# Packed attention and a SoLU layer: batch 1's Z from float16 halves, a new order of the steps, more unread matmuls

## The chip, the cores and the metric

The kernel runs on one core of a Trainium2 chip. The metric is the device time of one execution in microseconds. Three runs of the kernel before took 389.59 to 392.84 us, with a median of 391.43.

## The reference

Eight batches of eight heads attend twice: 32 packed queries to 576 keys, then 576 queries to the 32 packed rows. The result, 4608 tokens of 512 values, goes through a layer with SoLU and a layer norm. All arrays are float32.

```python
p_packed = sm_attn(p, k, v)            # softmax(p k^T / 8) v, per batch and head
x = sm_attn(q, p_packed, p_packed)     # then (tokens, heads * 64)
h = x @ w_in                           # 512 -> 1024
solu = h * softmax(h)
ln = (solu - mean) / sqrt(var + 1e-06) * g_ln
out = ln @ w_out                       # 1024 -> 512
```

## The kernel before

The second attention and the first layer are one product here: for each batch b, Z is the packed rows times w_in (`make_z`, steps z0 to z7), and h is the second softmax times Z. Every product of the token tiles runs on TensorE (PE) in float16 with a high and a low half of each operand and three of the four cross terms.

A batch takes these flows. `pack` (steps k) transposes the keys, takes scores, maximum and exponential, transposes the exponentials, multiplies by v and leaves the packed rows, transposed, with their size. `unpack` (q) does the second softmax and leaves its high and low half, a_h and a_l. `make_z` (z) leaves the two halves zh and zl of Z. Batch 0 and 1 turn keys and queries on PE (`transpose_pairs`), the others on VectorE (DVE). The 4608 tokens are 36 tiles of 128 (`token_tile`, t0 to t35): a product of 12 matmuls for h, then maximum, exponential, u = e h, mean, a high and a low half of the centred u, a transposing DMA (yT, issued by SyncE's queue, SP), and a product of 24 matmuls with w_out's halves wch and wcl in four steps, an eviction scaled by the row's norm, and a store.

The preparation reads w_in in four parts (load `lw`, conversion W) and w_out in four (`lo`, O), turns p (steps p) and g (`lg`, g), finds the size of the weights (N, S) and scales w_out's halves (C). In `make_z`, `ZP_BY` says for each batch how the product is made: '0' from float32 operands (L570), '1' from float16 halves of the packed rows and of w_in (L564, three terms). Batches 0 and 1 use float32 before, the others halves. The halves of w_in come from `weight_halves` (steps H): a high half per part on ScalarE (ACT, L342) and a low half per part on DVE (L344), written over the float32 w_in, so float32 products must be over first.

Two flows make matmuls that nobody reads: `warm_up` (Z) ahead of the first transposes and `keep_clock` (X), two matmuls of 384 columns in each of four steps.

Each flow is a Python generator, and a step is what lies between two `yield`s. The string `ORDER` names the flow whose next step is issued, 1316 names in all; the kernel issues in this order, so it fixes the order of the instructions on every engine and on SP's queue. The engines run their own instructions in that order and wait for each other by semaphores. Strings such as `SOFT_BY`, `A2L_BY`, `SCALED_BY` and `E1T_BY` choose the engine of single steps: d DVE, p or g GpSimd (POOL), a ACT. Three buffers of two banks each (`ps_h`, tile h) in PSUM serve transposes, scores, Z and h; one bank (po) serves the output product and the unread matmuls.

Of the kernel before, what the change touches and what calls it, by code (L numbers as in the profile page):

```python
# [12 lines left out]
ALU = mybir.AluOpType  # L13
# [4 lines left out]
SCALED_BY = 'gggggggg'  # L18
ZL_BY = 'ddpdpppdpppppppppppppppppppppppp'
A2L_BY = 'ddpppppppppppppp'  # L20
SOFT_BY = 'ppppppppdppppppp'
# [5 lines left out]
E1T_BY = 'aaaaaa'  # L27
# [4 lines left out]
ZP_BY = '00111111'  # L32
# [17 lines left out]
def packed_attention_solu_kernel(ctx: ExitStack, tc: tile.TileContext, q: bass.AP, k: bass.AP, v: bass.AP, p: bass.AP, w_in: bass.AP, w_out: bass.AP, g_ln: bass.AP, out: bass.AP):  # L50
    nc = tc.nc
# [3 lines left out]
    P = 128  # L55
# [59 lines left out]
    def warm_up():  # L115
        for _ in range(24):
            nc.tensor.matmul(spare[:, :P], lhsT=ones_f, rhs=ones_f, start=True, stop=True)
        for _ in range(15):
            nc.tensor.matmul(spare, lhsT=ones, rhs=ones.unsqueeze(1).broadcast_to([P, DM // P, P]), start=True, stop=True)
        yield  # L120

    def keep_clock():
        for _ in range(4):
            for _ in range(2):
                nc.tensor.matmul(spare[:, P:], lhsT=ones, rhs=ones.unsqueeze(1).broadcast_to([P, DM // P - 1, P]), start=True, stop=True)
            yield
# [206 lines left out]
    def weight_halves():  # L333
# [7 lines left out]
        for g in range(G):  # L341
            nc.scalar.activation(halves[0][g], w_in_sb[:, g], AF.Copy, scale=s_w)  # L342
            yield
            nc.vector.scalar_tensor_tensor(out=halves[1][g], in0=w_in_sb[:, g], scalar=s_w, in1=halves[0][g], op0=ALU.mult, op1=ALU.subtract)  # L344
            yield
# [422 lines left out]
```

## Time and profile before

| | us |
|---|---|
| median of three runs | 391.43 |
| the profiled execution | 391.56 |
| its span, first to last instruction | 389.7 |
| PE busy | 373.7 (96%) |
| DVE busy | 293.7 (75%) |
| ACT busy | 256.8 (66%) |
| POOL busy | 244.3 (63%) |
| mean granted TensorE clock | 0.981 |

The busy part of 40 equal slices, in tenths, and the clock that TensorE was granted, as a share of full speed:

```profile
PE   6858889999999999999999999999999999999996
...
DVE  2656879899997987778797679978767868475741
ACT  2566689797768687945857756844648559465740
...
PEclk9989779999999999999999999999999999999999
```

A slice is 9.7 us. The first six slices hold the preparation, in which PE is not full and the clock falls twice; from the seventh on PE is full to the last slice. A digit 9 is 90% or more. Busy matmuls overlap, so a full PE is read from its idle time.

### The profile page before, as it was taken

Reading aid. Unit: us, or ns where it says so; the run is one execution under the profiler, and the core shown is the slowest. Engines: PE = TensorE matmul, PEld = TensorE weight load, DVE = VectorE, ACT = ScalarE, POOL = GpSimd, SP = SyncE. Lnnn points to the kernel's source line nnn. Section 1 sums busy time; section 2 is a strip of 40 time slices with the busy share of each in tenths; the row PEclk is TensorE's granted clock in tenths of the full one; section 3 lists DMA queues with packets and bytes.
Section 4 is the critical chain, followed back from the end, with each engine's and each line's share of the span. In section 5 each row is a group of like instructions: output and inputs, shape, how many; then the busy total and the mean of one; then the engine's idle time right before and its main releaser. Section 6 shows DMA issues by size and latency. Waiting matters only on the chain.

```text
span 389.7 us, 8501 instructions
## 1 busy us (share of the span) xinstructions
PE 373.7 (96%) x3220; PEld 189.3 (49%) x3220; DVE 293.7 (75%) x472; ACT 256.8 (66%) x447; POOL 244.3 (63%) x410
## 2 busy tenths in 40 slices
PE   6858889999999999999999999999999999999996
PEld 6746345444545444544455445444455444444445
DVE  2656879899997987778797679978767868475741
ACT  2566689797768687945857756844648559465740
POOL 2673679887446987774456467785456767843550
PEclk9989779999999999999999999999999999999999
DMA  8999892898899999999987987973730535344361
GB/s 309 395 369 353 189 203 50 201 189 166 147 209 168 233 192 198 178 156 231 185 180 137 210 161 158 193 168 74 147 81 30 136 82 101 87 106 106 89 163 54
DMA packets 213017, 66.10 MB, mean 170 GB/s; under 512 B 192872, under 2 KB 206960, under 8 KB 212464
## 3 DMA queue, kind: packets, MB, share of 16 engines
q1 hardware_dynamic: 212976, 65.56, 74.4%
q8 instruction: 25, 0.41, 0.4%
q14 instruction: 16, 0.13, 0.1%
HBM read 37.23 MB, written 9.44 MB: 120 GB/s over the span
## 4 chain that ended last, share of the span: by engine, by line
PE 72%; DVE 3%; ACT 1%; DMA 1%; issue 1%; POOL 1%; SPq 0%; DVEq 0%; ACTq 0%
PE po L691 38%; PE h L631 19%; PE h L691 5%; PE h L564 2%; PE pa L432 2%; PE h L399 2%; PE h L516 1%; PE h L422 1%; DMA raw<-in_q_dram 1%; DVE u L656 1%; DVE nm L634 1%; ACT e L652 1%; DVE s L477 0%; DVE w_in_sb L344 0%; SPq L159 0%
## 5 line engine op out<-in xcount | busy, mean ns | idle before, releaser
L691 PE MATMUL po<-wch,yT 128*128 128x512 f16 x512 | 160.1, 379 | 0.1
L691 PEld LDWEIGHTS <-yT 128*128 128x128 f16 x888 | 85.9, 98 | 99.7 <-issue 4.9
L691 PE MATMUL po<-wcl,yT 128*128 128x512 f16 x256 | 97.0, 379 | 0.0
L656 DVE SCALAR_TENSOR_TENSOR u<-e,s_row,h 128x1024 f32<-128x1024 f32 x36 | 45.8, 1272 | 18.3 <-ACT e L652 12.9
L667 DVE SCALAR_TENSOR_TENSOR yhl<-u,negmu,yhl 128x1024 f16<-128x1024 f32 x36 | 47.5, 1319 | 4.7 <-ACT yhl L665 4.6
L634 DVE TENSOR_REDUCE nm<-h 128x1 f32<-128x1024 f32 x36 | 43.6, 1212 | 8.3 <-PE h L631 7.9
L631 PE MATMUL h<-zh,a_h 128*128 128x512 f16 (+2 forms) x168 | 47.7, 380 | 0.5 <-ACT qT L371 0.5
L631 PE MATMUL h<-zl,a_h 128*128 128x512 f16 (+2 forms) x168 | 47.9, 380 | 0.1
L652 ACT ACTIVATE e<-h,nmc,z_scale 128x1024 f32<-128x1024 f32 x36 | 43.2, 1200 | 1.9 <-PE h L631 0.8
L631 PEld LDWEIGHTS <-a_h 128*128 128x128 f16 (+2 forms) x336 | 27.7, 100 | 34.4 <-issue 5.0
L665 ACT ACTIVATE yhl<-u,negmu 128x1024 f16<-128x1024 f32 x36 | 41.1, 1145 | 0.7
L673 ACT ACTIVATE e<-u,negmu 128x1024 f32<-128x1024 f32 x36 | 41.0, 1138 | 0.0
L639 ACT ACTIVATE nmc<-nm,z_scale 128x1 f32<-128x1 f32 x33 | 9.6, 292 | 45.9 <-DVE nm L634 45.9
L642 POOL TENSOR_SCALAR bound<-nm,z_scale 128x1 f32<-128x1 f32 x33 | 12.9, 390 | 37.6 <-DVE nm L634 36.1
L680 POOL TENSOR_SCALAR c_row<-sq,s_eps 128x1 f32<-128x1 f32 x36 | 12.8, 355 | 29.3 <-ACT e L673 26.4
L631 PE MATMUL h<-zh,a_l 128*128 128x512 f16 (+2 forms) x84 | 30.4, 379 | 0.1
L631 PE MATMUL h<-zl,a_l 128*128 128x512 f16 (+2 forms) x84 | 30.4, 379 | 0.0
L699 DVE TENSOR_SCALAR o_sb<-po,c_row,inv 128x512 f32<-128x512 f32 x18 | 14.6, 810 | 13.7 <-PE po L691 6.9
L681 POOL TENSOR_TENSOR c_row<-c_row,neg_half 128x1 f32<-128x1 f32 x36 | 22.5, 626 | 3.0
L660 ACT ACTIVATE negmu<-su 128x1 f32<-128x1 f32 x36 | 7.2, 200 | 25.5 <-DVE u L656 25.4
L496 POOL TENSOR_TENSOR a<-a,sm 128x576 f32<-128x576 f32 x16 | 20.3, 1274 | 5.5 <-DVE sm L494 4.5
L532 POOL TENSOR_TENSOR a_l<-s,a_h 128x576 f16<-128x576 f32 x14 | 20.4, 1462 | 4.5 <-ACT a_h L530 4.5
(173 smaller groups left out, 684.6 us busy)
## 6 DMA issues: line engine op xcount, KB each, us to landing
out_dram<-o_sb SPq DMA_DIRECT2D x34, 256.0 KB, 2.4
v_sb<-in_v_dram SPq DMA_DIRECT2D x8, 1024.0 KB, 8.1
raw<-in_k_dram SPq DMA_DIRECT2D x24, 288.0 KB, 4.5
raw<-in_q_dram SPq DMA_DIRECT2D x96, 72.0 KB, 2.6
zh<-in_moe_w_in_dram SPq DMA_DIRECT2D x2, 1024.0 KB, 7.9
zl<-in_moe_w_in_dram SPq DMA_DIRECT2D x2, 1024.0 KB, 8.0
raw<-in_k_dram SPq DMA_DIRECT2D x2, 1024.0 KB, 11.6
raw<-in_moe_w_out_dram SPq DMA_DIRECT2D x2, 1024.0 KB, 8.3
```

Source lines behind the costliest of these rows:

```text
L496: EN(nc, SOFT_BY[2 * b + 1]).tensor_tensor(out=w2, in0=w2, in1=sm.unsqueeze(2).broadcast_to([P, NB, J]), op=ALU.mult)
L532: EN(nc, A2L_BY[2 * b + r]).tensor_tensor(out=lo, in0=a2T, in1=hi, op=ALU.subtract)
L631: nc.tensor.matmul(dst_[:, cols], lhsT=lhsT, rhs=z[:, r, cols], start=bool(first), stop=bool(last))
L634: nc.vector.tensor_reduce(out=nm, in_=h, axis=AX.X, op=ALU.max, negate=True)
L652: nc.scalar.activation(e, h, AF.Exp, bias=nmc, scale=sc[:, 1:], accum_out=se)
L656: nc.vector.scalar_tensor_tensor(out=u, in0=e, scalar=s_row, in1=h, op0=ALU.mult, op1=ALU.mult, accum_out=su)
L665: nc.scalar.activation(yhl[:, 0], u, AF.Identity, bias=negmu)
L667: nc.vector.scalar_tensor_tensor(out=yhl[:, 1], in0=u, scalar=negmu, in1=yhl[:, 0], op0=ALU.add, op1=ALU.subtract)
L673: nc.scalar.activation(e, u, AF.Square, bias=negmu, accum_out=sq)
L681: nc.gpsimd.tensor_tensor(out=c_row, in0=c_row, in1=neg_half, op=ALU.pow)
L691: nc.tensor.matmul(po[:, cols], lhsT=yT[:, a, c], rhs=w[:, c, cols], start=c == 0 and t == 0, stop=c == NFC - 1 and t == 2)
L699: nc.vector.tensor_scalar(out=o_sb[:, cols], in0=po[:, cols], scalar1=c_row, scalar2=inv, op0=ALU.mult, op1=ALU.mult)
```

## The change

Batch 1's Z is made from float16 halves (`ZP_BY`), so the steps H stand ahead of z1. `warm_up` is cut into 11 steps with the same matmuls, all issued at the same place. `keep_clock` has 11 steps in place of 4. In the preparation the steps of `ORDER` are the same up to tile 0's first product but for these: batch 0's first exponential, second score product and second maximum stand ahead of w_in's part 0; g's transpose stands behind the third step of p and two unread steps; seven unread steps are added; the first H moves behind. From tile 0 on the steps stand in a new order throughout. The names left in `ORDER` that issued nothing are gone. Single steps move from POOL to DVE: one low part of w_out (C6), softmax steps of batches 1 and 3 to 7 (`SOFT_BY` now has a letter for each half and step), low parts of a (`A2L_BY`); three copies of transposed exponentials move from ACT to DVE (`E1T_BY`). The new branch in `weight_halves` is not used (`HL_BY` is all d).

```diff
-SCALED_BY = 'gggggggg'
+SCALED_BY = 'ggggggdg'
-A2L_BY = 'ddpppppppppppppp'
-SOFT_BY = 'ppppppppdppppppp'
+A2L_BY = 'ddpppdddpppddpdp'
+SOFT_BY = 'ppppdpppppppddpddppddppppddpdpdd'
-E1T_BY = 'aaaaaa'
+E1T_BY = 'aaaaaaadadadaaaa'
-ZP_BY = '00111111'
+ZP_BY = '01111111'
+HL_BY = 'dddd'
     def warm_up():
-        for _ in range(24):
-            nc.tensor.matmul(spare[:, :P], lhsT=ones_f, rhs=ones_f, start=True, stop=True)
-        for _ in range(15):
-            nc.tensor.matmul(spare, lhsT=ones, rhs=ones.unsqueeze(1).broadcast_to([P, DM // P, P]), start=True, stop=True)
-        yield
+        for _ in range(6):
+            for _ in range(4):
+                nc.tensor.matmul(spare[:, :P], lhsT=ones_f, rhs=ones_f, start=True, stop=True)
+            yield
+        for _ in range(5):
+            for _ in range(3):
+                nc.tensor.matmul(spare, lhsT=ones, rhs=ones.unsqueeze(1).broadcast_to([P, DM // P, P]), start=True, stop=True)
+            yield
     def keep_clock():
-        for _ in range(4):
+        for _ in range(11):
...
-            copy_by(nc, E1T_BY[2 * b + i0 // 8] if b < 3 else 'a')(...)
+            copy_by(nc, E1T_BY[2 * b + i0 // 8])(...)
-            EN(nc, SOFT_BY[2 * b]).tensor_tensor(out=s2[r], ..., op=ALU.subtract)
+            EN(nc, SOFT_BY[4 * b + r]).tensor_tensor(out=s2[r], ..., op=ALU.subtract)
-            EN(nc, SOFT_BY[2 * b + 1]).tensor_tensor(out=w2, ..., op=ALU.mult)
+            EN(nc, SOFT_BY[4 * b + 2 + r]).tensor_tensor(out=w2, ..., op=ALU.mult)
```

`ORDER`, the preparation from the first unread steps to tile 0, and the steps from there to batch 1's product:

```diff
-... W2 X X k0 k0 lo1 W0 lq0 g W0 W0 k0 k0 W0 k0 p k0 k0 O0 W3 p lv0 ...
+... W2 X X k0 k0 lo1 k0 k0 k0 W0 lq0 W0 W0 W0 p X X k0 k0 O0 W3 g p lv0 ...
-... z0 X X q0 O3 O1 q0 O2 z0 k1 lk2 lq1 S z0 ... k1 z0 z0 S q0 q0 k1 q0 k1 k1 S k1 ... C3 H lk2 ... C3 q1 t0 C6 ...
+... z0 X X q0 O3 O1 q0 O2 z0 X k1 lk2 lq1 S X z0 ... k1 z0 X z0 S q0 q0 k1 q0 k1 X k1 S k1 ... C3 lk2 ... C3 q1 X t0 C6 ...
-k2 k1 k2 C4 k1 t0 C0 q1 t0 t0 t1 C3 k2 k1 k1 k2 k1 t1 lv1 C5 t0 C0 k1 t0 lk3 t0 C6 q1 k1 t1 lk3 k1 C0 t2 k1 t1 t0 ...
+k2 k1 k2 C4 k1 t0 C0 q1 t0 t0 t1 C3 t1 lk3 C6 lv1 C1 k2 k2 lk3 lk3 k1 C1 k1 k1 k1 lk3 C5 t0 t0 t0 k1 k1 lq2 C0 C0 t1 t1 lq2 k1 t0 t0 C1 t0 H H q1 t2 t2 t1 k1 k1 q1 H H t1 C7 t1 C7 q1 H H t3 ... z1 q1 q1 q1 t3 t2 t2 k2 k2 q1 t1 t1 t2 t1 H H k2 t1 t3 z1 k2 H z1 z1 q1 t2 ...
```

## Rows read from the trace of the kernel before

**Rows 1.** Page part 1: busy time, share of the span, instructions, by engine

```profile
PE 373.7 (96%) x3220; PEld 189.3 (49%) x3220; DVE 293.7 (75%) x472; ACT 256.8 (66%) x447; POOL 244.3 (63%) x410
```

**Rows 2.** Page part 4: the chain that ended last, shares by engine, by line

```profile
PE 72%; DVE 3%; ACT 1%; DMA 1%; issue 1%; POOL 1%; SPq 0%; DVEq 0%; ACTq 0%
PE po L691 38%; PE h L631 19%; PE h L691 5%; PE h L564 2%; PE pa L432 2%; PE h L399 2%; PE h L516 1%; PE h L422 1%; DMA raw<-in_q_dram 1%; DVE u L656 1%; DVE nm L634 1%; ACT e L652 1%; DVE s L477 0%; DVE w_in_sb L344 0%; SPq L159 0%
```

**Rows 3.** View by stretches: us, busy by engine, granted clock, DMA share, GB/s

```profile
27.00:31.00 4.00, 4.00 (x30) 3.67 (x29) 1.50 (x3) 1.70 (x4) 2.79 (x2) 0.57 1.11 323
44.00:54.00 10.00, 9.54 (x66) 4.08 (x58) 7.28 (x18) 7.53 (x14) 5.92 (x7) 0.51 0.97 203
23.00:26.00 3.00, 0.60 (x2) 0.41 (x3) 1.68 (x3) 2.97 (x8) 1.42 (x2) 1.00 1.10 375
41.00:44.00 3.00, 1.67 (x18) 1.28 (x18) 2.90 (x9) 2.63 (x3) 1.61 (x2) 1.00 0.97 321
57.00:110.00 53.00, 52.63 (x541) 24.76 (x547) 49.94 (x84) 42.49 (x77) 40.59 (x64) 1.00 0.83 151
110.00:380.00 270.00, 269.65 (x2199) 128.44 (x2184) 206.34 (x320) 179.38 (x319) 172.78 (x315) 1.00 0.71 148
```

**Rows 4.** Timeline of ACT: start, us, instruction, idle before it and its end

```profile
22.00 1.16 ACT L229 ACTIVATE e<-zh 128x1024 f32<-128x1024 f32 x1 [3.66 <-DMA zh<-in_moe_w_in_dram]
23.03 0.80 ACT L406 ACTIVATE e<-h,nmx 128x576 f32<-128x576 f32 x1
...
47.35 1.01 ACT L371 COPY kT<-h 128x1024 f32<-128x1024 f32 x1 [0.43 <-PE h L369]
...
49.83 0.37 ACT L378 COPY kT<-h 128x256 f32<-128x256 f32 x1 [1.26 <-PE h L376]
```

**Rows 5.** Timeline of SP, and the landing of v's loads by tile view

```profile
22.40 0.43 SPq L133 DMA_DIRECT2D v_sb<-in_v_dram  x1
...
DMA to landing us min/median/max: 7.3/8.3/8.7
```

**Rows 6.** Timeline of PE before the token tiles

```profile
20.56 0.22 PE L186 MATMUL po<-ident,g_raw 8*128 8x8 f32 x1 [1.46 <-DMA g_raw<-in_moe_g_ln_dram]
...
31.58 1.45 PE L432 MATMUL pa<-v_sb,e1T 128*32 128x64 f32 x80
...
39.32 0.97 PE L125 MATMUL po<-ones 128*128 128x384 f32 x4
...
41.86 1.06 PE L369 MATMUL h<-ident,raw 128*128 128x128 f32 x8 [0.58 <-PE h L570]
...
43.80 1.61 PE L570 MATMUL h<-w_in_sb,ppT 64*32 64x512 f32 x8 [0.75 <-DVE zh L580]
...
56.02 0.59 PE L631 MATMUL h<-zh,a_h 128*128 128x512 f16 x2 [0.48 <-ACT qT L371]
```

**Rows 7.** Z's products: timeline of PE, then chain in order of time (batch 3)

```profile
78.00 1.92 PE L570 MATMUL h<-w_in_sb,ppT 64*32 64x512 f32 x24
...
80.57 1.06 PE L570 MATMUL h<-w_in_sb,ppT 64*32 64x512 f32 x8
...
148.72 1.42 PE h L564 x48
```

**Rows 8.** Batch 2's operand on DVE and the product's first matmuls on PE

```profile
108.98 0.35 DVE L553 SCALAR_TENSOR_TENSOR pph<-ppT,s_p,pph 128x128 f16<-128x128 f32 x1
...
109.79 0.41 PE L564 MATMUL h<-w_hi,pph 64*32 64x512 f16 x8
```

**Rows 9.** View by line and shape: count | busy us, mean ns | idle before

```profile
L344 DVE SCALAR_TENSOR_TENSOR w_in_sb<-w_in_sb,s_w,w_hi 128x1024 f16<-128x1024 f32 x4 | 5.0, 1256 | 0.0
...
L553 DVE SCALAR_TENSOR_TENSOR pph<-ppT,s_p,pph 128x128 f16<-128x128 f32 x6 | 3.1, 509 | 0.0
...
L580 DVE SCALAR_TENSOR_TENSOR zh<-h,z_scale,zh 128x512 f16<-128x512 f32 x4 | 3.0, 744 | 0.0
...
L483 DVE TENSOR_TENSOR s<-s,mx 128x576 f32<-128x576 f32 x2 | 1.4, 754 | 0.0
```

More of the change, by code (lines that the diff above doesn't have):

```diff
@@ L343, in weight_halves @@
             yield
-            nc.vector.scalar_tensor_tensor(out=halves[1][g], in0=w_in_sb[:, g], scalar=s_w, in1=halves[0][g], op0=ALU.mult, op1=ALU.subtract)
+            if HL_BY[g] == 'd':
+                nc.vector.scalar_tensor_tensor(out=halves[1][g], in0=w_in_sb[:, g], scalar=s_w, in1=halves[0][g], op0=ALU.mult, op1=ALU.subtract)
+            else:
+                nc.gpsimd.tensor_scalar(out=w_in_sb[:, g], in0=w_in_sb[:, g], scalar1=s_w, scalar2=0.0, op0=ALU.mult, op1=ALU.add)
+                nc.gpsimd.tensor_tensor(out=halves[1][g], in0=w_in_sb[:, g], in1=halves[0][g], op=ALU.subtract)
             yield
@@ L423, in pack @@
             yield
-            copy_by(nc, E1T_BY[2 * b + i0 // 8] if b < 3 else 'a')(e1T[:, i0:i0 + len(grp)], pt[:, :len(grp) * P].rearrange('p (i j) -> p i j', j=P))
+            copy_by(nc, E1T_BY[2 * b + i0 // 8])(e1T[:, i0:i0 + len(grp)], pt[:, :len(grp) * P].rearrange('p (i j) -> p i j', j=P))
             yield
@@ L482, in softmax @@
             yield
-            EN(nc, SOFT_BY[2 * b]).tensor_tensor(out=s2[r], in0=s2[r], in1=mx.unsqueeze(2).broadcast_to([P, NB, J]), op=ALU.subtract)
+            EN(nc, SOFT_BY[4 * b + r]).tensor_tensor(out=s2[r], in0=s2[r], in1=mx.unsqueeze(2).broadcast_to([P, NB, J]), op=ALU.subtract)
             yield
@@ L495, in softmax @@
             yield
-            EN(nc, SOFT_BY[2 * b + 1]).tensor_tensor(out=w2, in0=w2, in1=sm.unsqueeze(2).broadcast_to([P, NB, J]), op=ALU.mult)
+            EN(nc, SOFT_BY[4 * b + 2 + r]).tensor_tensor(out=w2, in0=w2, in1=sm.unsqueeze(2).broadcast_to([P, NB, J]), op=ALU.mult)
             a2.append(w2)
```

2 lines of the change are left out of this document (1 added, 1 removed).

## The prediction

> **What bounds the kernel now.** I read the busy shares first. TensorE (PE) is busy 96% of the span and the next engine far less [rows 1], and the chain of waits runs through PE for 72% of it, mostly through the two products of the token tiles [rows 2]. A share over the whole span hides two stages, so I cut it with the view by stretches [rows 3]. From 110 to 380 us PE is busy 269.65 of 270 us at full clock and VectorE (DVE) only 206.34: there the time is PE's work and nothing else. From 57 to 110 us PE is busy 52.63 of 53 us, but DVE 49.94 as well. Two engines are full at once, and DVE has only 3.1 us to spare. Before 57 us PE waits. Its stream of token tiles begins at 56.02 us, and the wait in front of it ended on a ScalarE (ACT) copy [rows 6].
>
> So the end is the start of tile 0's first product, plus PE's work behind it, plus any wait of PE behind it, of which there is next to none now. The change can act on these three terms only. The sum is made against the profiled execution, 391.56 us (span 389.7, and 1.86 around it), which is 0.13 above the median of 391.43.
>
> **The start of the token tiles.** (1) Batch 0's first exponential on ACT stands behind the conversion of a w_in part that waits for its load until 22.00 us; it starts at 23.03 and takes 0.80 [rows 4]. The new order puts it ahead of that wait, into ACT's idle time, so its 0.80 us goes. The second exponential stays behind the same conversion and moves up by no more. What is late next is v of batch 0: its load is issued at 22.40 and the longest landing of such a load is 8.7 us, so 31.1 us by estimate, and the product with v starts at 31.58 now [rows 5, 6]. Only 0.5 of the 0.80 fits; I take 0.5, ends 0 and 0.8. (2) g's transpose made PE wait 1.46 us for its load, with batch 0's second score product queued behind it [rows 6]. That score product now goes first, but its exponential is the one still held by ACT's 22.00 us load, so this edit is costed at nothing; if that load came sooner, it would be worth up to 1.46. (3) Seven more steps of unread matmuls. Two steps together took 0.97 us with their drain [rows 6], so one is 0.49 at most and seven are 3.4 us if nothing hid them. The third and fourth fall into the wait before batch 0's first transposes of exponentials, where PE was busy 0.60 of 3 us [rows 3]; the seventh and eighth into waits of 0.58 and 0.75 us [rows 6]; the tenth and eleventh stand ahead of scores and of tile 0, where PE waits for ACT anyway (0.48 before tile 0 [rows 6]). Only the ninth, ahead of batch 1's last transposes, has no cover: 0.49.
>
> What the steps change is the clock. In 44 to 54 us the granted clock averages 0.51, the lower of its two levels (1.2 against 2.4 GHz), while PE is busy nearly throughout; before it fell, PE had been busy 1.67 of 3 us. In 27 to 31 us it averages 0.57, after 0.60 of 3 us busy [rows 3]. At full clock PE would do the 44 to 54 work in about half the time, but what runs there waits for ACT and DVE too. What a faster PE gives back is the idle time of ACT that PE ended there: 0.43 us at 47.35 and 1.26 us at 49.83, 1.69 together [rows 4]. Less the ninth step this is 1.2; ends 0 (the clock falls all the same) and 1.69. I take 1.2, because the seventh to ninth steps fill just the gaps in front of the fall. For the first dip I take nothing, since two steps there still leave PE waiting; its upper end is the 43% of 4 us that the clock withheld, 1.7 us.
>
> On this clock the Trainium skill ("TensorE: Matmul & The Clock Gate", Part 4) says that transposes do not engage the full clock as matmuls do. By it only the unread steps could hold the clock, and term (3) would be its upper end, 1.69. The trace agrees in part: the clock stayed low through a busy stretch with many transposes, yet it rose at the end of that stretch without any unread step.
>
> Start of the tiles: 0.5 + 1.2 = 1.7 us sooner.
>
> **PE's work behind the start.** Batch 1's Z took 1.92 us for 24 and 1.06 us for 8 float32 matmuls, about 2.9 with the overlapped drain taken off; a batch from halves takes 1.42 [rows 7]. That is 1.5 us less on PE, all of it in the saturated part. No other matmul is added or removed there.
>
> **PE's waits behind the start.** Here the change pays. Batch 1's product now needs the float16 halves of w_in, so four ACT copies and four DVE subtractions of 1.256 us each [rows 9] are brought ahead of it. Before, the product ran at 78.00 [rows 7] with none of those subtractions needed, and they were spread up to batch 2's product. On PE the second score steps, batch 2's further work and the tiles' output products are queued behind that product. The halves are not new work, they are moved; tile steps of DVE move behind them. New on DVE before batch 2's Z are one low part of w_out moved from GpSimd (nearest row 0.744), one subtraction of batch 1's softmax (0.754), and the low half of the packed operand (0.509) [rows 9]: 2.0 us. Batch 2's product is a good place to weigh both engines, since both versions have the same work behind it: DVE finished its operand at 109.33 and PE began at 109.79, a slack of 0.46 [rows 8]. With PE 1.5 us lighter and DVE 2.0 us heavier, PE would wait 1.5 + 2.0 - 0.46 = 3.0 us. DVE has 3.1 us of idle time in 57 to 110 [rows 3], some of which the moved subtractions can fill; I take half, 1.5, ends 0 and 3.1. So PE waits 1.5 us (0 to 3.0), and the 1.5 us of lighter work is lost again.
>
> **Costed at nothing:** the further softmax and attention steps moved from GpSimd to DVE, 6 low parts, 9 softmax steps, 3 small copies from ACT, 18 instructions at about 0.75 us or less, 13 us. They lie behind 110 us, where DVE has 63.7 us idle in 270 [rows 3]; without that cover they would cost up to 13. The warm-up is cut into more steps with the same matmuls in the same place. Loads and stores move on SyncE's queue with their tiles: batch 3's k and part of batch 2's q now stand ahead of tile 0's transposing DMA. They wait for buffers that come free before tile 0's low half is ready, so they should be past; if not, tile 0's output product is late by one such issue. The new order of the later tiles keeps PE fed as long as DVE's spare holds; a tile's output product just in time costs some tenths, below what I can weigh, either way.
>
> **Sum:** 391.56 - 1.7 - 1.5 + 1.5 = 389.9 us in a profiled execution, 389.8 against the median.
>
> **Rivals.** (a) *All of it arrives.* Both clock dips go (1.7 + 1.7), and DVE's idle time takes its added work, so PE never waits: 391.56 - 1.7 - 1.7 - 1.5 = 386.7 us. For it: DVE's 3.1 us idle would just do. Against: waits of an engine in order seldom fill fully. (b) *The preparation gains nothing.* The unread steps do not hold the clock, or loads set the pace (v, k): 391.56 - 1.5 + 1.5 = 391.6. For it: v's half microsecond of room, and DVE busy 2.90 of the 3 us in 41 to 44 [rows 3]. (c) *The new wait in front of batch 1's product decides.* PE comes to it before the last low half of w_in, nothing of DVE's idle time helps, and PE waits 3.0 us there; after such a wait the clock falls as it did after 23 to 26 and 41 to 44. The two dips withheld 1.7 and 4.9 us of PE work [rows 3], their mean 3.3. Then 391.56 - 1.7 - 1.5 + 3.0 + 3.3 = 394.7, slower than before. With the clock fallen, the two gains (3.2) are spent by the 3.3 alone and every wait comes on top; so it decides as soon as a wait there brings the clock down. The Trainium skill ("TensorE: Matmul & The Clock Gate", Part 1) also has the clock fall when PE idles between bursts; nothing behind 57 us in this trace shows it, for PE never idled there.
>
> **How the numbers follow.** Forecast 0.40, (a) 0.25, (b) 0.20, (c) 0.15. About 1%, 3.9 us, is what a measurement of this kernel can tell from no change. Faster by more than that is below 387.5: most of (a), a little of the forecast, 0.24. Slower by more is above 395.3: half of (c) and a little of the rest, 0.09. The rest, 0.67, lies within. The range goes from 386.0, (a) with the upper ends of (1) and (3), 0.3 and 0.49 more, to 393.8, into (c): some 0.1 is left out at each end. The forecast alone, with its ends, would be 388 to 391.8.
>
> **What would show it.** Right: the first exponential before 22 us; no stretch at the lower clock from 44 to 54; tile 0's first product at 54.3 instead of 56.02; 48 float16 matmuls of 1.42 us for batch 1; a wait of PE for VectorE of 1 to 2 us in front of batch 1's or batch 2's product, and none from 110 us on. Wrong: tile 0 starting where it did; or PE idle again and again behind 110 us, by which DVE's added work would not be covered; or a lower clock behind 57 us.

## The result: 1.2% slower

The changed kernel took 395.82 us (median of four runs, 393.98 to 396.44), the kernel before 390.51 beside it. The ratio is 1.0124, with a 95% interval from 1.0075 to 1.0173. The forecast was 389.8, and the range ended at 393.8: the time lies outside, on the other side of the kernel before. In two of the experiments below some runs were slow ones (one of six, three of twelve): their ratios are of the fast runs alone, their medians of all.

The profiled execution of the changed kernel is its fastest run: 393.98 us, with a span of 392.2. Its busy times on the page (against [rows 1]):

```profile
PE 373.4 (95%) x3250; PEld 189.9 (48%) x3250; DVE 307.8 (78%) x494; ACT 258.6 (66%) x445; POOL 220.1 (56%) x392
```

PE does as much as before in a longer span. The stretches that stood in [rows 3], in the changed kernel (us, busy by engine, granted clock, DMA share, GB/s):

```profile
27.00:31.00 4.00, 4.00 (x34) 3.67 (x30) 2.12 (x3) 1.75 (x4) 3.11 (x2) 0.67 1.10 327
44.00:54.00 10.00, 7.79 (x81) 4.30 (x74) 8.70 (x20) 9.69 (x17) 7.61 (x6) 1.00 1.00 191
57.00:110.00 53.00, 50.13 (x588) 24.25 (x586) 50.69 (x87) 43.02 (x77) 33.80 (x59) 1.00 0.88 174
110.00:380.00 270.00, 268.42 (x2158) 126.53 (x2143) 216.34 (x336) 178.57 (x312) 153.50 (x300) 1.00 0.67 141
```

Up to 54 us it went as forecast: no lower clock from 44 to 54, and the first dip stays. Behind that, PE is idle 2.87 of 53 us where it was idle 0.37, and 1.58 of 270 us where it was 0.35. The places, in PE's timeline (start, us, instruction, idle before it and what ended it):

```profile
53.93 0.59 PE L639 MATMUL h<-zh,a_h 128*128 128x512 f16 x2 [0.68 <-ACT qT L379]
...
61.90 1.32 PE L440 MATMUL pa<-v_sb,e1T 128*32 128x64 f32 x80 [1.16 <-ACT e1T L432]
...
67.28 0.72 PE L512 MATMUL h<-qT,ppT 64*32 64x288 f32 x16 [0.62 <-DVE ppT L456]
...
69.64 0.39 PE L699 MATMUL po<-wch,yT 128*128 128x512 f16 x1 [0.24 <-DMA yT<-yhl]
...
79.28 1.11 PE L430 MATMUL h<-ident,e 128*128 128x128 f32 x7 [0.54 <-ACT e L414]
...
85.72 0.41 PE L572 MATMUL h<-w_hi,pph 64*32 64x512 f16 x8
...
99.57 0.35 PE L462 MATMUL pa<-total,ones_f 128*128 128x1 f32 x2 [0.31 <-DVE ppT L456]
...
212.30 0.72 PE L407 MATMUL h<-kT,pT 64*32 64x288 f32 x16 [0.31 <-DVE u L664]
217.55 0.35 PE L462 MATMUL pa<-total,ones_f 128*128 128x1 f32 x2 [0.47 <-DVE ppT L456]
243.44 0.33 PE L446 MATMUL pa<-ident,pp 128*128 128x128 f32 x1 [0.42 <-DVE pp L443]
254.65 0.40 PE L639 MATMUL h<-zh,a_h 128*64 128x512 f16 x1 [0.33 <-DVE u L664]
385.96 0.27 PE L699 MATMUL h<-wch,yT 128*128 128x256 f16 x1 [0.69 <-DVE o_sb L707]
```

Tile 0 starts at 53.93 us instead of 56.02, batch 1's product at 85.72 waits for nothing, and ten small waits lie behind the start: 1.16 + 0.62 + 0.24 + 0.54 + 0.31 + 0.31 + 0.47 + 0.42 + 0.33 + 0.69 = 5.1 us. From tile 0's start to PE's last end it is 330.3 us before (56.02 to 386.34) and 334.8 now (53.93 to 388.74). PE is busy 329.6 and 329.5 us of that, although batch 1's product is lighter by 1.5 us. A wait also costs an overlap of two matmuls: two in a row take 0.59 us and one alone 0.39 (rows above), so one that follows without a gap adds some 0.2. By this estimate it is some 0.2 us for each wait, 2 us for the ten.

### The profile page after: what moved, and what is told of

Its sections match the earlier page's. It is cut to its first block, busy times and chain, and to the rows that moved or that the text cites. A ratio compares the mean times of both kernels' runs of the same rounds, so it can differ in the third digit from the quotient of the medians.

```text
span 392.2 us, 8517 instructions
## 1 busy us (share of the span) xinstructions
PE 373.4 (95%) x3250; PEld 189.9 (48%) x3250; DVE 307.8 (78%) x494; ACT 258.6 (66%) x445; POOL 220.1 (56%) x392
## 5 line engine op out<-in xcount | busy, mean ns | idle before, releaser
L650 POOL TENSOR_SCALAR bound<-nm,z_scale 128x1 f32<-128x1 f32 x33 | 14.3, 434 | 53.1 <-DVE nm L642 50.9
L689 POOL TENSOR_TENSOR c_row<-c_row,neg_half 128x1 f32<-128x1 f32 x36 | 21.5, 598 | 3.0
L639 PEld LDWEIGHTS <-a_l 128*128 128x128 f16 (+2 forms) x168 | 14.3, 99 | 17.3 <-DVE a_l L540 0.6
L699 PE MATMUL h<-wch,yT 128*128 128x512 f16 (+1 forms) x80 | 20.5, 336 | 0.7 <-DVE o_sb L707 0.7
L656 POOL TENSOR_TENSOR s_row<-bound,neg_one 128x1 f32<-128x1 f32 x33 | 19.0, 576 | 2.7
```

The source lines that it names most:

```text
L639: nc.tensor.matmul(dst_[:, cols], lhsT=lhsT, rhs=z[:, r, cols], start=bool(first), stop=bool(last))
L650: by.tensor_scalar(out=bound, in0=nm, scalar1=-1.0 / U_MAX, scalar2=sc[:, :1], op0=ALU.mult, op1=ALU.max)
L656: nc.gpsimd.tensor_tensor(out=s_row, in0=bound, in1=neg_one, op=ALU.pow)
L689: nc.gpsimd.tensor_tensor(out=c_row, in0=c_row, in1=neg_half, op=ALU.pow)
L699: nc.tensor.matmul(po[:, cols], lhsT=yT[:, a, c], rhs=w[:, c, cols], start=c == 0 and t == 0, stop=c == NFC - 1 and t == 2)
```

## Experiments

Each ratio is against the kernel before, run beside it. Its median in the five groups of runs was 389.87 to 391.31, so the ratios are compared, not the times.

**The two halves of the change.** Only the preparation, up to tile 0's first product:

```diff
-ORDER = '<changed>'
+ORDER = '<changed, up to C3 q1 X, with H back behind C2 C3> <before, from the first t0 on>'
-ZP_BY = '01111111'
+ZP_BY = '00111111'
 # SCALED_BY, A2L_BY, SOFT_BY, E1T_BY as before
```

> The changed preparation (unread steps, first exponential sooner, g later) with everything behind tile 0's first product as it was before: order of the tiles, engines, batch 1's Z from float32. Tile 0 should start at 53.9 us, as in the changed kernel, instead of 56.02. Theory 'new order': the 2.1 us reach the end, 390.51 - 2.1 = 388.4 us (ratio 0.995), and all that makes the changed kernel slower is behind the start. Rival 'chain': batch 1's chain through ScalarE and VectorE, not PE, sets the pace from 60 to 80 us, so PE waits there instead and the time stays at 390.5 (1.000).

Measured: 390.06 us, ratio 0.9992 [0.9976, 1.0009]. No gain clear of noise, but the chain is not the reason: from 60 to 80 us this kernel's PE is busy 19.85 of 20 us. The profile of the other half says more:

```diff
-ORDER = '<changed>'
+ORDER = '<before, up to C3 q1, without H> <changed, from the first t0 on>'
 # warm_up and keep_clock as before
```

> The preparation as it was before, and behind tile 0's first product the changed order, the changed engines and batch 1's Z from halves. Theory 'new order': the order costs by itself what the changed kernel lost and the preparation's 2.1 us besides, 395.8 + 2.1 = 397.9 us (ratio 1.019). Rival 'chain': the start is waited away by batch 1's chain in the changed kernel, so a later start costs little, 395.8 (1.014).

Measured: 395.60 us, 1.0139 [1.0112, 1.0165], about the whole loss. Its preparation is the old one. Its stretches, and tile 0's start in PE's timeline:

```profile
44.00:50.00 6.00, 4.15 (x45) 1.72 (x38) 4.87 (x15) 5.43 (x10) 4.30 (x5) 1.00 0.93 164
50.00:53.30 3.30, 3.30 (x28) 2.05 (x27) 3.30 (x6) 3.30 (x7) 2.50 (x3) 0.50 1.10 189
```

```profile
54.27 0.59 PE L636 MATMUL h<-zh,a_h 128*128 128x512 f16 x2 [0.24 <-ACT qT L376]
...
71.99 0.39 PE L696 MATMUL po<-wch,yT 128*128 128x512 f16 x1 [2.25 <-DMA yT<-yhl]
```

The same old preparation kept the full clock (2.4 GHz) until 50 us and had the lower one (1.2 GHz) for 3.3 us instead of ten. It started tile 0 at 54.27, not 56.02. So the execution that I had priced was one with a long fall. What the new steps cure is not lost in every execution.

The 88 runs of the kernel before that stand beside the experiments show how often. In 18 the mean granted clock was 0.972 to 0.978 and the median time 393.0 us, in 24 it was 0.981 to 0.983 and 391.3 us, in 46 it was 0.986 or more and 389.7 us. The execution that I priced (0.981) is of the middle group. With the changed preparation the clock was 0.991 or more in all twelve runs, and the time 389.1 to 390.7 us. So the preparation does prevent the long falls, but it saves nothing where there is none; its own profile has three waits of PE behind tile 0's start (0.15, 0.66 and 0.48 us).

**VectorE's added work.** Softmax steps, low parts and copies back on GpSimd and ScalarE, in the changed order:

```diff
-A2L_BY = 'ddpppdddpppddpdp'
+A2L_BY = 'ddpppppppppppppp'
-SOFT_BY = 'ppppdpppppppddpddppddppppddpdpdd'
+SOFT_BY = 'ppppppppppppppppddpppppppppppppp'
-E1T_BY = 'aaaaaaadadadaaaa'
+E1T_BY = 'aaaaaaaaaaaaaaaa'
```

> The changed kernel with the softmax steps, the attention's low parts and the copies of exponentials back on GpSimd and ScalarE, 17 of the instructions that had gone to VectorE, some 12 us; the order stays. Theory 'VectorE's load': PE's waits for VectorE behind 60 us (about 3.5 us by the list of waits, with those in the windows 200 to 220 and 240 to 260) go for the most part, 395.8 - 2.5 = 393.3 us (ratio 1.007). Rival 'order': the waits come from where the steps stand, so the time stays within 0.5 of 395.8 (1.014).

Measured: 399.70 us, 1.0233 [1.0204, 1.0263]: slower than the changed kernel. New waits of PE take the place of the old:

```profile
161.80 0.38 PE L699 MATMUL po<-wch,yT 128*128 128x512 f16 x1 [0.87 <-ACT o_sb L705]
168.29 1.32 PE L440 MATMUL pa<-v_sb,e1T 128*32 128x64 f32 x80 [1.15 <-ACT e1T L432]
178.76 0.40 PE L639 MATMUL h<-zh,a_h 128*64 128x512 f16 x1 [1.50 <-DVE s L485]
...
218.02 1.32 PE L440 MATMUL pa<-v_sb,e1T 128*32 128x64 f32 x80 [1.87 <-ACT e1T L432]
```

Nineteen instructions went back, not 17: DVE has 475 in this profile and 494 in the changed kernel's. Of the five waits behind 110 us, three are gone from this trace (0.31, 0.42, 0.33), but larger ones for ScalarE's copies and the softmax stand in their place. So the new order needs those steps on DVE, and taking DVE's added load away doesn't bring the loss back.

**The tail.**

```diff
-... t34 t35 t35 t35 t33 t35 t34 t35 t35 t35 t35 t35 t34 t35'
+... t35 t35 t35 t33 t35 t35 t34 t34 t34 t35 t35 t35 t35 t35'
```

> The changed kernel with the last steps of tiles 34 and 35 as before: the last quarter of tile 34's output product stands between the two halves of tile 35's again. The wait of 0.7 us between those halves goes: 395.8 - 0.7 = 395.1 us (ratio 1.012). If the wait was covered by the last eviction and store anyway, 395.8.

Measured: 394.31 us, 1.0102 [1.0071, 1.0134]. The wait between the halves is gone from its trace; 0.0022 of 390.5 us is 0.9, near the 0.7 expected, and inside both intervals.

**Where in the order.** The changed order up to the first step of batch 2's Z, and before's behind it:

```diff
-ORDER = '<changed>'
+ORDER = '<changed, up to the first z2> <the rest, in the order of before>'
 # SOFT_BY, A2L_BY, E1T_BY as before from batch 2 on
```

> The changed order and engines up to the first step of batch 2's Z (about 110 us), with batch 1's Z from halves, and behind it the order and engines of before. Theory 'steps before their inputs': the waits that PE shows in that stretch (1.16 for the copy of batch 1's exponentials, 0.62 and 0.31 for its packed operand, 2.3 for the transposing DMA, 0.54 for an exponential, 0.3 at the start) are 5.2 us, less the 1.5 us of Z, against 390.1 for the preparation alone: 393.8 us (ratio 1.009). Rival 'the loss is behind 110 us': 390.1 - 1.5 = 388.6 (0.996).

Measured: 392.38 us, 1.0044 [1.0017, 1.0071]. From 1.0124 to 1.0044 is 3.1 us that the order behind 110 us costs, together with its engines; the intervals leave some 2 us either way. Against the preparation alone (0.9992) the early part costs 2.0 us net of the lighter Z. The reverse:

```diff
-ORDER = '<changed>'
+ORDER = '<changed preparation> <before, up to the first z2> <the rest, in the changed order>'
-ZP_BY = '01111111'
+ZP_BY = '00111111'
```

> The order and engines of before up to the first step of batch 2's Z, with batch 1's Z from float32, and the changed order and engines behind it. Theory 'steps before their inputs': the waits shown behind 110 us (0.31, 0.47 to 2.19, 0.42, 0.33, and 0.69 between the halves of the last output product) are 2.2 to 3.9 us: 390.1 + 2.2 = 392.3 us (ratio 1.005), up to 394. Rival 'the loss is ahead of 110 us': 390.1 (1.000).

Measured: 400.62 us, 1.0257 [1.0223, 1.029]. It does not answer: at the joint PE waits 5.04 us for a transposing DMA (113.79 us), which neither kernel has, and behind it the granted clock is 0.50 from 114 to 117 us. The later waits are there as in the changed kernel (0.30, 0.47, 0.41, 0.30 and 0.7 us).

The wait of 0.47 us is longer in other profiles of this late order: 2.19 us in the kernel with the mended tail, 0.81, 1.42 and 1.73 in three of the runs below. There (PE, then DVE):

```profile
220.85 0.35 PE L462 MATMUL pa<-total,ones_f 128*128 128x1 f32 x2 [2.19 <-DVE ppT L456]
```

```profile
219.75 0.78 DVE L391 STREAM_TRANSPOSE qT<-raw 128x576 f32<-128x576 f32 x1 [3.35 <-DMA raw<-in_q_dram]
220.46 0.25 DVE L456 COPY ppT<-pa 128x128 f32<-128x128 f32 x1
```

The copy that PE waits for stands in DVE's queue behind a transposition of q, and DVE waits 3.35 us for that load (1.96 to 2.89 in the other three, 0.93 in the changed kernel's profile, nothing in the kernel before). So what this wait has beyond 0.47 us is for a load, and not for DVE's work. The 0.47 us are the hand-over itself: in the changed kernel the copy starts 0.04 us after PE's product ends, and no step of PE stands between that product and the matmul that needs the copy.

**Batch 1's halves in the old order**, behind the changed preparation.

```diff
-... t2 z1 t2 H q1 z1 k2 t3 t1 z1 q1 lq3 H t1 t1 q1 k2 t2 t1 q1 q1 H q1 t1 z1 k2 k2 ...
+... t2 z1 t2 H H q1 k2 t3 H t1 q1 lq3 H t1 t1 H q1 k2 t2 H t1 q1 q1 H q1 t1 H z1 z1 z1 k2 k2 ...
-ZP_BY = '00111111'
+ZP_BY = '01111111'
```

> The changed preparation, the order and engines of before, and batch 1's Z from halves alone: the steps that make w_in's halves are brought ahead of it, and the product stands eight tile steps later. If PE's 1.5 us of lighter work arrives: 390.1 - 1.5 = 388.6 us (ratio 0.996). If VectorE's moved work takes it back, as the prediction has it: 390.1 (1.000). If PE comes to the product before the last low half: up to 3 us more, 393.

Measured: 398.74 us, 1.021 [1.0175, 1.0246]. PE waits for the halves, then the clock falls (PE's timeline, then stretches):

```profile
84.30 0.40 PE L572 MATMUL h<-w_hi,pph 64*32 64x512 f16 x5 [0.75 <-ACT w_hi L346]
85.61 0.37 PE L572 MATMUL h<-w_in_sb,pph 64*32 64x512 f16 x1 [0.90 <-DVE w_in_sb L349]
87.89 0.62 PE L572 MATMUL h<-w_in_sb,pph 64*32 64x512 f16 x5 [1.90 <-DVE w_in_sb L349]
```

```profile
84.00:90.00 6.00, 2.89 (x45) 0.91 (x44) 3.77 (x5) 0.25 (x1) 3.25 (x5) 0.74 0.41 67
90.00:94.00 4.00, 2.20 (x14) 1.99 (x10) 1.68 (x3) 3.65 (x6) 1.08 (x3) 0.50 0.05 22
```

This is rival (c), though in the old order (waits of 3.55 us, where it had 3.0): the halves brought ahead without moving what else ScalarE and VectorE have to do there. The Trainium skill ("TensorE: Matmul & The Clock Gate", Part 1) has the clock fall when PE idles between bursts; this trace agrees (0.50 behind a stretch with 2.89 of 6 us busy), and the changed kernel shows that short gaps can stay free: it lost 2.6 of 20 us at 60 to 80 us at a clock of 1.00.

**The transposing DMA of tile 0.** PE's wait for it is 0.24 us in the changed kernel's profile, but 2.25 above and 2.52 in the kernel with the mended tail; that may be most of the 1.8 us by which the profiled run lies under its median, of whose runs only one was profiled. In the mended tail's profile, SyncE's queue, the landing by tile view, and ScalarE's timeline:

```profile
60.65 5.06 SPq L163 DMA_DIRECT2D raw<-in_q_dram  x8
65.81 1.77 SPq L678 DMA_TRANSPOSE yT<-yhl  x1
```

```profile
DMA to landing us min/median/max: 5.4/5.4/5.4
```

```profile
71.26 1.15 ACT L673 ACTIVATE yhl<-u,negmu 128x1024 f16<-128x1024 f32 x1 [3.07 <-DMA yT<-yhl]
```

The kernel before, SyncE and PE:

```profile
61.71 1.93 SPq L159 DMA_DIRECT2D raw<-in_q_dram  x4
66.67 1.72 SPq L670 DMA_TRANSPOSE yT<-yhl  x1
```

```profile
72.72 0.39 PE L691 MATMUL po<-wch,yT 128*128 128x512 f16 x1
```

Tile 0's low half was ready at 64.12 us (DVE: 62.80 + 1.32), but SyncE was still issuing eight loads of q and came to the DMA at 65.81, 1.7 us late. The landing took 5.4 us, 1.5 more than the 3.9 before; why is open. Before, four loads stood there, and SyncE issued it at 66.67, 0.06 us after its low half. ScalarE waits too, since tile 1's yhl goes into the buffer that this DMA reads. Before, ScalarE came to tile 1's yhl at 72.20, after the landing (66.67 + 3.9); here it is there at 68.2. To move the loads behind the DMA:

```diff
-... t1 lk3 C6 lv1 C1 k2 k2 lk3 lk3 k1 ... k1 lk3 C5 ... k1 lq2 ... t1 lq2 k1 t0 t0 C1 ...
+... t1 lk3 C6 C1 k2 k2 k1 ... k1 C5 ... k1 ... t1 k1 t0 t0 lv1 lk3 lk3 lk3 lq2 lq2 C1 ...
```

> The changed kernel with six loads (three parts of batch 3's k, batch 1's v, two parts of batch 2's q) moved behind tile 0's transposing DMA on SyncE, nothing else. Theory 'loads ahead': that DMA lands late because these loads are before it, and PE's wait of 2.25 and 2.52 us in front of tile 0's output product (in the two profiles that have it; 0.24 in the third) goes: 395.8 - 2.2 = 393.6 us (ratio 1.008). Rival: the landing takes as long without them, or another wait takes its place: 395.8 (1.014).

Measured: 406.50 us, 1.0423 [1.0388, 1.0458]. This kernel also moved batch 1's v behind its use, so that its product takes what the buffer held; its time says nothing of the mend. But it shows SyncE's queue at work (SyncE, then PE):

```profile
82.02 5.81 SPq L678 DMA_TRANSPOSE yT<-yhl  x1
```

```profile
90.00 0.61 PE L699 MATMUL po<-wch,yT 128*128 128x512 f16 x1 [10.88 <-DMA yT<-yhl]
```

The moved loads now stood ahead of tile 1's DMA, which was issued at 82.02 (72.65 in the changed kernel), and PE waited 10.88 us. Next, PE's own steps:

```diff
-... t3 k1 q1 q1 t0 t0 t3 t2 lv2 ... t3 k1 q1 t0 t0 t3 ...
+... t3 k1 q1 q1 t0 t3 t2 lv2 ... t3 k1 q1 t0 t0 t0 t3 ...
```

> The changed kernel with one step moved: the first quarter of tile 0's output product stands behind tile 3's second half and batch 1's second score product instead of ahead of them, 2.3 us of PE's work. The load order on SyncE is as changed. Theory 'steps before their inputs': PE only came to that product too soon, the transposing DMA lands as it does, and the wait of 2.3 us goes: 395.8 - 2.2 = 393.6 us (ratio 1.008). Rival 'the DMA is late, whatever PE does': PE waits in the next place, 395.8 (1.014).

Measured: 397.20 us, 1.0154 [1.0098, 1.021]: no gain. The wait moved to the step behind, and behind it the clock fell (PE, then a stretch):

```profile
73.60 0.38 PE L462 MATMUL pa<-total,ones_f 128*128 128x1 f32 x2 [2.73 <-ACT squares L460]
```

```profile
74.00:77.00 3.00, 3.00 (x21) 0.88 (x22) 2.90 (x7) 2.97 (x6) 2.61 (x6) 0.50 1.02 85
```

Batch 1's squares stand in ScalarE's queue behind tile 1's yhl, which waited 2.01 us for the DMA here. PE's busy time from tile 0's start is 331.2 us, 1.6 more than in the changed kernel: by estimate that is what the clock takes in this profile. The two runs of the highest clock (0.995 and 0.996) took 395.20 and 396.11 us, no less than the changed kernel. Two more steps moved:

```diff
-... t1 C3 t1 lk3 ... k1 C1 k1 k1 k1 lk3 ... q1 t2 t2 t1 k1 k1 q1 ...
+... t1 C3 lk3 ... k1 C1 k1 k1 t1 k1 lk3 ... q1 t2 t1 k1 t2 k1 q1 ...
```

> As the run before, and two more steps of PE moved: tile 1's second half stands between batch 1's transposes of exponentials and their product with v (covers 1.16 us), tile 2's second half between the transposes of batch 1's packed operand and its first score product (covers 0.62 us). Nothing of VectorE's, ScalarE's or SyncE's order is changed. Theory 'steps before their inputs': 393.6 - 1.7 = 391.9 us (ratio 1.004). Rival 'the chain of batch 1 sets the pace': the waits move on to the steps behind, and the time stays at 393.6 (1.008).

Measured: 397.98 us, 1.0149 [1.0091, 1.0206]: no gain either; PE waits 3.04 us there, and the clock falls behind it as above (0.50 from 74 to 77 us). The same three moves before the old late order, and with the mended tail:

> The changed order up to the first step of batch 2's Z with those three steps moved, and the order and engines of before behind it. That order without the three moves took 392.4. Theory 'steps before their inputs': 392.4 - 3.9 = 388.5 us (ratio 0.996), which leaves the 1.5 us of batch 1's lighter Z under the preparation alone (390.1) and beats both kernels. Rival 'chain': 391 to 392.4 (1.003).

> The changed kernel with the three steps moved and the last steps of tiles 34 and 35 as before. Theory 'steps before their inputs': 391.9 - 0.7 = 391.2 us (ratio 1.002); what stays above 388.5 are the waits of 0.3 to 0.5 us at 200 to 260 us. Rival 'chain': 392.9 or more (1.007).

Measured: 393.09 us, 1.0054 [1.0019, 1.0088], against 1.0044 without the moves; and 396.60 us, 1.0142 [1.0094, 1.019]. The first theory found no gain in four runs. A wait that is moved off one step of PE comes back at the next that needs ScalarE. In three of the four profiles the clock fell behind it, in the third behind a wait of 2.03 us (0.52 from 73 to 76 us), so these runs weigh the moves and the fall together. The fourth has a wait of 1.95 us, no fall, and took 394.03 us against the 391.2 expected.

**ScalarE's queue.** The last part of w_out scaled sooner, so that tile 1's yhl takes the other buffer:

```diff
-... t0 t0 C1 t0 H H ... t1 C7 t1 C7 ... t2 C7 t1 ...
+... t0 t0 C1 t0 C7 C7 C7 H H ... t1 t1 ... t2 t1 ...
```

> The changed kernel with the three steps of w_out's last part (a ScalarE step and two of GpSimd) moved ahead of the first casts of w_in's halves, so that its buffer is given back before tile 1's yhl is placed. Theory 'buffer': ScalarE's wait for tile 0's transposing DMA (0.79 to 3.07 us) goes or falls to 0.5, and with it what stands behind it in ScalarE's queue comes sooner; PE's wait of 2.3 us for the DMA itself, in front of tile 0's output product, stays, since PE comes there no later: 394.5 to 395.8 us (ratio 1.011 to 1.014). Rival 'halves': ScalarE is late because of the casts of w_in's halves, with or without that wait: no change, 395.8, and the wait moves to the next step of ScalarE.

Measured: 396.87 us, 1.0139 [1.0107, 1.0171]. The wait for the DMA is gone on ScalarE and on PE. In its place ScalarE waits for GpSimd, and PE for ScalarE's copy of q, which stands behind the moved step of 0.7 us:

```profile
69.99 1.15 ACT L673 ACTIVATE yhl<-u,negmu 128x1024 f16<-128x1024 f32 x1 [0.97 <-POOL wcl L317]
```

```profile
67.93 0.72 PE L512 MATMUL h<-qT,ppT 64*32 64x288 f32 x16 [1.13 <-ACT qT L386]
```

With the three moves, in the changed kernel and with the old late order:

> The run before and the three PE steps moved. Theory 'buffer': now batch 1's size is not behind ScalarE's wait any more, and PE's waits of 2 to 3 us at 70 to 74 us go: 397.2 with the three steps alone becomes 393.5 (ratio 1.008). Rival 'halves': 396 or more (1.014).

> The order of the run before up to the first step of batch 2's Z, behind it the order and engines of before. Theory 'buffer': 393.1 without the buffer's part, less the 2.0 us wait for batch 1's size: 391.0 (ratio 1.001); if the small waits go with it 389.5 (0.997). Rival 'halves': 392.5 to 393 (1.005).

Measured: 395.79 us, 1.0107 [1.0076, 1.0137]; and 391.88 us, 1.0013 [0.9994, 1.0033]. Both are 0.4% under the same orders without this edit, but the intervals overlap. The second is as fast as the kernel before, with 1.5 us less work on PE; waits of PE eat that (0.68, 1.04, 1.20, 0.54 and 0.29 us in its trace). All its runs had a clock of 0.990 or more; against the runs of the kernel before that had no long fall (389.7 us) it is 2 us slower. Two of the waits:

```profile
67.27 0.72 PE L512 MATMUL h<-qT,ppT 64*32 64x288 f32 x16 [1.04 <-ACT qT L386]
71.88 0.38 PE L462 MATMUL pa<-total,ones_f 128*128 128x1 f32 x2 [1.20 <-ACT squares L460]
```

Loads of q behind tile 0's DMA:

```diff
-... k1 lq2 C0 C0 t1 t1 lq2 k1 t0 t0 C1 ...
+... k1 C0 C0 t1 t1 k1 t0 t0 lq2 lq2 C1 ...
```

> The run before with two loads of batch 2's q (eight issues of 0.62 us on SyncE) behind tile 0's transposing DMA. If those issues make that DMA late it starts up to 1.2 us sooner, and what still waits for it gains as much: 390 (ratio 0.999). If nothing waits for it any more, as early_best.

Measured: 394.06 us, 1.0070 [1.0036, 1.0105], slower. Its one profile, of a run of 398.32 us, has the waits of the run before and one more:

```profile
94.06 0.61 PE L699 MATMUL po<-wch,yT 128*128 128x512 f16 x1 [3.62 <-DMA yT<-yhl]
```

The moved loads now stand between the first two transposing DMAs; the second took SyncE 5.29 us to issue (1.63 in the run before), and the third was issued at 88.45 us instead of 84.08. Behind the wait the clock is 0.50 from 94 to 98 us. Whether the faster runs have a shorter form of this was not profiled. Last, the halves taken out of the stretch again:

```diff
-... t0 H H q1 ... H H t1 ... H H t3 ... t1 H H k2 t1 t3 z1 k2 H z1 z1 ...
+... t0 H q1 ... t1 ... t3 ... t1 k2 t1 t3 z1 k2 z1 z1 <eight H, spread up to the first z2> ...
-ZP_BY = '01111111'
+ZP_BY = '00111111'
```

> The changed kernel with batch 1's Z from float32 again and eight of the nine steps that make w_in's halves moved behind it, spread up to batch 2's Z; nothing else. PE's work rises by 1.5 us. Theory 'halves': the casts at 65 to 72 us made ScalarE late, and the waits at 66 to 75 us (0.6 to 1.1 for batch 1's packed operand, 2.3 to 2.5 for the transposing DMA and what stands behind it) go for the most part: 395.8 + 1.5 - 3 = 394.3 us (ratio 1.010). Rival 'order': the waits stay and the product costs its 1.5 more: 397.3 (1.018).

> The mended early order (w_out's last part sooner, three PE steps moved, behind batch 2's Z as before), with batch 1's Z from float32 and the halves made behind it as in the run beside it. Theory 'halves': its waits of 1.04 (copy of q) and 1.2 us (squares) go, 1.0013 + (1.5 - 2.2) / 391 = ratio 0.9995, no slower than the preparation alone (0.9992). Rival 'order': they stay, and the product costs its 1.5 more: ratio 1.005.

Measured: 400.04 us, 1.0235 [1.0175, 1.0294]; and 394.22 us, 1.0083 [1.0055, 1.0112]. Both are slower than with the halves, by more than the product's 1.5 us (0.0038). In the first the wait for the DMA stays, on PE and on ScalarE:

```profile
70.88 0.39 PE L699 MATMUL po<-wch,yT 128*128 128x512 f16 x1 [2.43 <-DMA yT<-yhl]
```

```profile
70.92 1.15 ACT L673 ACTIVATE yhl<-u,negmu 128x1024 f16<-128x1024 f32 x1 [4.95 <-DMA yT<-yhl]
```

So the DMA's wait comes without the halves too: it is the order's. In the second, PE's waits at 67 to 72 us fall from 1.04 + 1.20 to one of 0.36, so there the halves did hold ScalarE; but where they are made now, PE waits again, and the product costs its 1.5 us:

```profile
70.99 0.38 PE L462 MATMUL pa<-total,ones_f 128*128 128x1 f32 x2 [0.36 <-ACT squares L460]
101.80 0.35 PE L462 MATMUL pa<-total,ones_f 128*128 128x1 f32 x2 [1.50 <-DVE ppT L456]
...
114.21 0.38 PE L699 MATMUL po<-wch,yT 128*128 128x512 f16 x1 [0.98 <-ACT o_sb L705]
```

No version beats the kernel before by more than the measurement can tell.

## Why the prediction was wrong, step by step

- **The start, 1.7 us sooner.** Each mechanism was right in the trace: the first exponential at 21.66 us (23.03 before), the product with v at 31.17 (31.58), no fall of the clock in 44 to 54, tile 0 at 53.93 where I had 54.3. The size was wrong: the preparation alone gave 0.08%, 0.3 us, within noise. Term (3) was priced on one execution whose clock was low for ten us; another execution of the same steps had 3.3 us of it, and 46 of the 88 runs above have next to nothing to give back.
- **Batch 1's product, 1.5 us lighter.** It began without a wait, its 48 matmuls took from 85.72 to 87.14 us, 1.42 as forecast, and no other matmul was added or removed behind the start. It holds.
- **1.5 us of waits for DVE before batch 1's or batch 2's product.** Wrong in place and engine: neither product waits in the changed kernel. The early part lost 3.5 us in place of the 1.5 (2.0 net and the 1.5 of Z), at hand-overs from ScalarE, DVE and the transposing DMA. Bringing the halves ahead was counted on DVE alone; their four casts also load ScalarE, which has batch 1's copies and squares in the same stretch. In the mended early order that was 1.9 us of PE's waits (1.04 + 1.20 - 0.36).
- **The moved instructions, nothing.** Right in sign: without them the new order is 0.0109 slower.
- **The loads on SyncE, nothing, "so they should be past".** This failed. In the trace of the mended tail SyncE reached tile 0's DMA 1.7 us late, it landed 1.5 us more slowly, and PE came to it 4.0 us sooner than before (at 68.70, where its 2.52 us wait began, against 72.72). The slack of that DMA was gone: 0.2 to 2.5 us of waits on PE, 0.4 to 4.95 on ScalarE, over the profiles. The run that was to take the loads away (1.0423) is no test of it.
- **The order of the later tiles, "some tenths, below what I can weigh".** This is the step that failed most: "keeps PE fed as long as DVE's spare holds" was given no price, and it cost 3.1 us behind 110 us (0.0080), of which the tail is about 0.9. DVE had spare there (216.34 of 270 us busy), and PE still waited. Five waits of 0.31 to 0.69 us stand there, one of them 0.81 to 2.19 in other profiles. All five end on DVE, but the one that grows does so for a load of q that lands late, as shown above, and the last is the eviction between two halves of a product. The other three were not taken apart, and the reverse order (1.0257) did not confirm the sum: the place is shown, the cause only in part.

Put together, in the terms of the forecast (-1.7 - 1.5 + 1.5 + 0 = -1.7 us): -0.3 - 1.5 + 3.5 + 3.1 = 4.8 us. Two of its bounds are added up wrongly: the forecast's own ends give 387.6 to 393.1 us, not 388 to 391.8, and the range starts at 385.9. The measured time is outside all the same.

My "wrong if" said it: PE idle again and again behind 110 us. But it blamed DVE's added work, and the run without that work is slower still. Rival (c) gave the nearest number (394.7), but its mechanism is not the changed kernel's: batch 1's product does not wait there, and the clock stays at 1.00 behind 57 us. That it comes near is luck.

## What to carry to other kernels

An order that keeps the bottleneck engine idle 0.1% of the time is itself the tuned thing: price a new one by its slack at each hand-over (DMA landing, buffer, copy), on every engine that the moved steps load, not by busy shares. A gain read from the clock of one execution needs more executions before it goes into a sum; the mean clock that each run lists is enough. And moving the step that waits does not help while another engine's queue is what is late: several short waits can become one long one, behind which the clock falls.

## What the runs showed of the hardware that was not expected

One program's preparation is not one time: the same 24 warm-up matmuls took 6.14 to 7.66 us in the profiles, and with the new preparation tile 0 started from 52.98 to 54.55 us, not in step with the warm-up (6.35 and 54.28 in one, 7.09 and 53.24 in another). The time of the kernel before goes with the clock that a run was granted (389.7 us at 0.986 or more, 393.0 at 0.978 or less). Behind single waits of PE of 2.03, 2.73 and 3.04 us the clock fell, behind others of 2.25, 2.33, 2.43 and 2.52 us it did not. Tile 0's transposing DMA took 3.8 to 5.6 us to land; SyncE spent 1.5 to 6.3 us on issuing such a DMA.
